# Attention and two feed-forward blocks on one core: when v and the adding transfers are issued, twelve matmuls into an idle bank, and bank locks handed back a slot later

## The chip, the cores and the metric

The kernel runs on one core of one Trainium2 chip. A core has five engines with a queue each, worked off in order: TensorE (PE, with its weight loads as PEld), VectorE (DVE), ScalarE (ACT), GpSimd (POOL) and SyncE (SP, which here only issues transfers). SP and POOL issue transfers that 16 DMA engines carry out. The metric is the device time of one execution in microseconds; lower is better.

## The reference, cut to what matters

```python
# q, k, v: (4, 8, 576, 64)
q_d, k_d, v_d = means of 4 neighbouring positions             # 144 positions
out_d     = softmax(q_d @ k_d.T / 8) @ v_d                    # coarse attention
out_local = softmax(q @ k.T / 8 where |i - j| < 4) @ v        # local attention
x  = out_d repeated 4 times + out_local                       # (4, 576, 512)
xn = (x - mean) / sqrt(var + 1e-6) * g_ln
x  = x + relu(xn @ w_ch1) @ w_ch2                             # 512 -> 2048 -> 512
xp = x shifted by one position
k  = relu((mu_k*x + (1-mu_k)*xp) @ w_k)                       # 512 -> 1024
out = sigmoid((mu_r*x + (1-mu_r)*xp) @ w_r) * ((k*k) @ w_v)   # 1024 -> 512
```

Everything is float32. The kernel keeps that precision in matmuls of a faster 32-bit type by splitting each factor into a high and a low part and adding three products (high·high, high·low, low·high): `mm3`, lines 203 to 206.

## The kernel before, in words

The 2304 positions are cut into six chunks of 384 columns, c = 0 to 5. The first half of the program goes through the chunks with the first feed-forward block (layer 1 into the banks `h_ps`, layer 2 into the four banks `acc0` to `acc3`, 16 slices f of the hidden size, 384 matmuls in a chunk). The attention of chunk c+1 is woven into the matmuls of chunk c: `slot` is called four times per slice and lets the generators in `Attn` advance by a budget. The second half (lines 773 to 837) is the second feed-forward block.

Attention of a chunk is four units (c, hp), hp being a pair of heads. A unit loads q and the windows of k (`load_qk`, tile `kz`) and the windows of v (`load_v`, tile `v`, two buffers), makes scores (coarse ones `scd`, local ones `sc`), softmaxes, transposes (`tp`, `PT`, `PdT`), multiplies with v (`av`), and adds both parts into `x`. At most two units are alive at a time. The bank `av` is shared by `scd`, `tp`, `av` and `var`; the list `av_user` in the generator is a lock on it.

The coarse k and v of a batch are sums over four neighbouring positions. For batch 0 they are made by DVE (`first_k`, tile `kf`) and POOL (`first_v`, tile `vr`). For the other batches `sums` loads one of the four parts with a transfer by SP and adds the other three with accumulating transfers issued by POOL, each of which waits until the one before it has landed (tiles `kd`, `vd`, seven buffers, lines 243 to 249). There are 12 such chains of three steps, each step a pair kd and vd: 36 pairs.

The weights come as 64-bit floats. `conv_gen` loads 32 pieces of 512 KB (`raw`, line 124, or line 129 for the last four), turns them into 32-bit floats and splits them: for each piece ACT at lines 80, 84 and 88, DVE at lines 81, 85 and 91. Piece n has to be split before the layer slice that uses it. All of it happens in front of and during chunk 0. Attention of chunk 0 has no matmuls to hide behind: it, with the first weights, is the prologue, and layer 1 of chunk 0 begins when its `x` is normalised (`xc`, `ah`, `al`).

At the end of a chunk `emit_x2` scales the four banks by the norm (`x2t`, DVE, two buffers), adds them to `x` (POOL, line 610) and stores the chunk to memory (`x2d`, one transfer of SP, line 611).

The order on each queue is set by a scheduler from its own estimate of when things are ready; an instruction given to `in_order` (line 67) keeps its place in program order among others so marked. Since queues are worked off in order, an instruction that waits holds up everything behind it on its engine. A name such as (1, 2) below is the unit hp = 2 of chunk 1.

Of the kernel before, what the change touches and what calls it, by code (L numbers as in the profile page):

```python
# [8 lines left out]
F32 = mybir.dt.float32  # L9
# [29 lines left out]
def tile_block(ctx: ExitStack, tc: tile.TileContext, qw, kw, kf, kr, vw, vr, vec, mask, w1, w2, wk, wv, wr, out):  # L39
# [27 lines left out]
    def in_order(on, ins):  # L67
        if on:
            tc.keep_in_program_order(ins)
# [37 lines left out]
    def conv_gen():  # L107
# [4 lines left out]
        def fetch():  # L112
            key = next(todo, None)
            while key in raws:
                key = next(todo, None)
            if key is None:
                return
            nm, p, k = key
            src = w1s[:, :, 1024 * p:1024 * p + 1024] if nm == "w1" else w2s[:, 4 * p:4 * p + 4, :]
            t = wpool.tile([128, 2, 1024], I32, tag="w", name="raw")  # L120
            for i in range(2):
                raws[nm, p, k + i] = t[:, i]
            for i in range(2):
                in_order(len(raws) < 18, nc.sync.dma_start(t[:, i], src[:, k + i]))

# [12 lines left out]
        for n, key in enumerate(keys + [None]):  # L138
            pin = n < PINNED
            if last:  # L140
                in_order(pin, split_hi(h, w))
            if key:
                nm, p, k = key
                W = W1 if nm == "w1" else W2
                if p not in W:
                    W[p] = wtiles(f"{nm}_{p}")
                g = decode(raws[key], pin)
                w1st = next(g)
            yield
            if key:  # L150
                next(g, None)
            if last:
                in_order(pin, split_lo(h, l, w))
                done.add(last)
            if key:
                h, l, w = W[p][0][:, k, :], W[p][1][:, k, :], w1st
            last = key
            if n % 2 == 1 or n > 24:
                fetch()
            if n + 1 < len(keys):  # L160
                fetch_late(keys[n + 1])
            yield
# [47 lines left out]
    loaded, kds, vdt, vts = {}, {}, {}, {}  # L210
    qds, adding, firsts, raw_k, means = {}, {}, [], {}, {}
    xt, xsum, stage = {}, {}, {}
# [28 lines left out]
    def sums(c, hp):  # L241

        new = [(b, *sum_tiles(b, hp)) for b in dict.fromkeys(runs(c)) if (b, hp) not in kds]
        for r in range(4):
            for b, kd, vd in new:
                eng, op = (nc.gpsimd, {"accum_op": ALU.add}) if r else (nc.sync, {})
                in_order(c <= 1 and r > 0, eng.dma_start(kd, kr[b, hp, r], **op))  # L247
                in_order(c <= 1 and r > 0, eng.dma_start(vd, vr[b, hp, r], **op))  # L248
            yield

# [15 lines left out]
    def prep(c, hp):  # L266
# [9 lines left out]
        qds[c, hp] = qd  # L276

    def mean_of(c, hp):
        if hp == 0:
# [3 lines left out]
    def unit(c, hp, nxt):  # L283
        if (c, hp) not in qds:
            prep(c, hp)
        if nxt is not None:
            if nxt not in loaded:
                load_qk(*nxt)
                if nxt[0] == 0:
                    first_k(nxt[1])  # L290
            if nxt not in vts:
                load_v(*nxt)
                if nxt[0] == 0:
                    first_v(nxt[1])
        i = units.index((c, hp)) + 2
        far = units[i] if i < len(units) else None
        if far is not None and far not in adding:
            adding[far] = sums(*far)
        step = lambda: next(adding[far], None) if far is not None else None
        step()  # L300
        new = c == 0 or runs(c)[1] != runs(c - 1)[1]
        q, k = loaded.pop((c, hp))
        v = vts.pop((c, hp))
        if hp == 0:
# [41 lines left out]
        for j in range(2):  # L346
            nc.scalar.activation(Pd[:, j, :], scd[:, j, :], AF.Exp, bias=m[:, j:j + 1], scale=0.125 / 16.0, accum_out=sm[0:2 * QB, 2 * NG + j:2 * NG + j + 1])  # L347
        if c > 0:
            av_user.clear()
        elif nxt in loaded:  # L350
            prep(*nxt)
        yield 900
        stage[c, hp] = 1
        step()
        nc.vector.tensor_reduce(mx[:, 0:2 * NG], Pl, axis=AX.X, op=ALU.max)
# [10 lines left out]
        yield 400  # L366
        step()
        nc.vector.tensor_reduce(sm[:, 0:2 * NG], P[:, :, 0:WIN + 1], axis=AX.X, op=ALU.add)
# [4 lines left out]
        while c + hp > 0 and units[units.index((c, hp)) - 1] not in multiplied:  # L373
            yield GAP
        step()
        T = pat.tile([128, 2 * NG, 32], F32, tag="T", name="T", bufs=1)
# [21 lines left out]
        if c == 0 and hp > 0:  # L398
            mean_of(c, hp - 1)
        av = ps_at.tile([128, 512], F32, tag="av", name="av")  # L400
        for n in range(NG):
# [26 lines left out]
        if c == 0:  # L428
            if hp == NHP - 1:
                mean_of(c, hp)  # L430
        elif hp == 1:
            xsum[c] = pln.tile([128, N], F32, tag="xsum", name="xsum")
# [51 lines left out]
    def scale(c):  # L484
# [26 lines left out]
        nc.vector.tensor_scalar(ve, var[:, 0:N], 1e-6, None, op0=ALU.add)  # L511
        nc.scalar.activation(t, ve, AF.Ln)
        av_user.clear()
        yield 400
        nc.scalar.activation(y, t, AF.Exp, scale=-0.5)
# [88 lines left out]
    def emit_x2(c):  # L604
        x = xt.pop(c)
        y = rstd.pop(c)
        for o in range(KT):
            t = xp.tile([128, N], F32, tag="x2", name="x2t")
            nc.vector.tensor_tensor(t, acc[o][:, 0:N], y, op=ALU.mult)  # L609
            nc.gpsimd.tensor_tensor(x[:, o, :], t, x[:, o, :], op=ALU.add)  # L610
        nc.sync.dma_start(x2d[:, :, N * c:N * c + N], x)

# [39 lines left out]
    for o in ORDER:  # L652
# [9 lines left out]
        else:  # L662
            next(conv)
    adding.update((u, iter(())) for u in units[0:NHP])
    first = Attn(None, 0)
# [244 lines left out]
```

## Time and profile before

| what | value |
|---|---|
| median of 3 runs | 795.38 us (795.38 to 796.32) |
| profiled execution | 795.89 us |
| its span, first to last instruction | 794.1 us |
| PE busy | 752.4 us, 95% of the span |
| DVE busy | 513.0 us, 65% |
| ACT busy | 370.7 us, 47% |
| POOL busy | 99.3 us, 13% |
| mean granted clock of TensorE | 0.987 of full |

Busy shares are means over stages that differ. The prologue takes the first 54 us, chunk 0 ends at about 152 us, chunk 5 at about 540 us, and the second block fills the rest. In the rows, a time at the start of a row is its start from the beginning of the span, the next number its duration; in square brackets stands how long the engine had been idle before it and what it had waited for. "SPq" is the issue of a transfer by SP. PEclk is the granted clock as a share of full speed: 1.00 is 2.4 GHz, 0.50 is 1.2 GHz.

### The profile page before, as it was taken

The page shows a single profiled execution, that of the slowest core. Times are in us where ns is not written, and L with a number is a line of the kernel's source. Part 1 is how long each engine was busy: PE and PEld are TensorE (multiplying, and loading weights), DVE is VectorE, ACT ScalarE, POOL GpSimd, SP SyncE. Part 2 cuts the span into 40 slices and gives each one's busy share as a digit, 9 for nine tenths or more (in the row PEclk, how much of TensorE's full clock was granted, in tenths as well). Part 3 has the DMA queues.
Part 4 walks back from the last instruction along what each step waited for, and adds up shares of the span by engine and source line. Part 5 has one row for each costly group of instructions (what it writes and reads, how often), then busy time and mean ns, then how long its engine had stood idle before and what let it go on. Part 6 is the DMA issues. An engine that isn't in the chain of part 4 may idle for free.

```text
span 794.1 us, 13626 instructions
## 1 busy us (share of the span) xinstructions
PE 752.4 (95%) x5380; PEld 722.6 (91%) x5380; DVE 513.0 (65%) x1015; ACT 370.7 (47%) x839; POOL 99.3 (13%) x124
## 2 busy tenths in 40 slices
PE   3669979899999999999999999999999999999998
PEld 2449869799999999999999999999999999999998
DVE  6777688766546655655555446625969596868664
ACT  4577587645434453445345324524444353525140
POOL 2334123413340001110100010001000000000000
PEclk9969999999999999999999999999999999999999
DMA  8894786446633421553134003403020202010101
GB/s 242 248 249 85 217 232 167 118 139 169 161 71 129 128 96 67 145 138 100 67 101 142 1 1 133 133 1 120 6 75 11 70 1 80 1 40 1 41 1 40
DMA packets 49023, 78.79 MB, mean 99 GB/s; under 512 B 5568, under 2 KB 34880, under 8 KB 48960
## 3 DMA queue, kind: packets, MB, share of 16 engines
q1 hardware_dynamic: 40320, 72.61, 29.0%
q0 software_dynamic: 8640, 5.32, 5.1%
q8 instruction: 42, 0.69, 0.3%
q14 instruction: 21, 0.17, 0.1%
HBM read 63.22 MB, written 14.68 MB: 98 GB/s over the span
## 4 chain that ended last, share of the span: by engine, by line
PE 83%; DMA 5%; ACT 5%; DVE 4%; issue 1%; SPq 1%; POOL 0%; ACTq 0%; POOLq 0%
PE b_ps L206 11%; PE b_ps L204 10%; PE b_ps L205 10%; PE h_ps L204 8%; PE h_ps L205 7%; PE h_ps L206 7%; PE acc L204 7%; PE acc L205 7%; PE acc L206 7%; PE av L403 2%; DMA raw<-in_w 2%; PE scd L333 1%; DMA vd<-in_vr 1%; DMA q<-in_qw 1%; PE sc L337 1%; ACT PT L381 1%
## 5 line engine op out<-in xcount | busy, mean ns | idle before, releaser
L590 DVE SCALAR_TENSOR_TENSOR hl<-h_ps,hh 128x384 fp32r<-128x384 f32 x96 | 53.0, 553 | 94.3 <-ACT hh L589 94.0
L589 ACT ACTIVATE hh<-h_ps 128x384 fp32r<-128x384 f32 x96 | 46.9, 489 | 104.3 <-PE h_ps L206 103.9
L206 PE MATMUL b_ps<-k,wbl 128*128 128x384 f32 x192 | 64.1, 334 | 0.0
L204 PE MATMUL b_ps<-xk,wbh 128*128 128x384 f32 x192 | 64.1, 334 | 0.0
L205 PE MATMUL b_ps<-xk,wbh 128*128 128x384 f32 x192 | 64.1, 334 | 0.0
L206 PE MATMUL b_ps<-xk,wbl 128*128 128x384 f32 x192 | 64.1, 334 | 0.0
L204 PE MATMUL b_ps<-k,wbh 128*128 128x384 f32 x192 | 64.1, 334 | 0.0
L205 PE MATMUL b_ps<-k,wbh 128*128 128x384 f32 x192 | 64.1, 334 | 0.0
L820 DVE RECIPROCAL e<-e 128x384 f32<-128x384 f32 x24 | 61.1, 2544 | 0.1
L610 POOL TENSOR_TENSOR x<-x2t,x 128x384 f32<-128x384 f32 x24 | 23.9, 1058 | 254.4 <-DVE x2t L609 132.2
L737 ACT ACTIVATE mixa<-x2in,vec_t 128x384 f32<-128x384 f32 x48 | 28.1, 612 | 39.7 <-DVE xr L740 33.9
L248 POOL DMA_DIRECT2D vd<-in_vr x36 | 35.1, 991 | 90.9 <-DMA vd<-in_vr 74.1
L381 ACT COPY PT<-T 32x192 f32<-32x192 f32 x96 | 33.4, 348 | 25.5 <-DVE T L377 22.9
L247 POOL DMA_DIRECT2D kd<-in_kr x36 | 35.6, 1013 | 65.8 <-DMA kd<-in_kr 60.0
L800 ACT ACTIVATE kr<-b_ps 128x384 f32<-128x384 f32 x48 | 23.5, 490 | 43.5 <-PE b_ps L206 43.5
L85 DVE SCALAR_TENSOR_TENSOR rm<-rm 128x512 uint32<-128x512 uint32 x52 | 35.7, 688 | 11.2 <-ACT rm L84 10.4
L801 DVE TENSOR_TENSOR kr<-kr,b_ps 128x384 f32<-128x384 f32 x48 | 26.5, 553 | 23.4 <-ACT kr L800 23.4
L84 ACT ACTIVATE rm<-raw 128x512 uint8<-128x512 uint8 x52 | 40.5, 784 | 2.1 <-DVE rm L81 1.9
L790 DVE TENSOR_TENSOR k<-kr,k 128x384 fp32r<-128x384 f32 x48 | 26.7, 557 | 20.3 <-ACT k L789 20.3
L347 ACT ACTIVATE Pd<-scd,mx 96x144 f32<-96x144 f32 x48 | 17.7, 372 | 44.2 <-DVE mx L344 43.7
L80 ACT ACTIVATE rm<-raw 128x512 f32<-128x512 f32 x52 | 34.3, 662 | 6.0 <-DMA raw<-in_w 5.7
L204 PE MATMUL h_ps<-ah,w_2h 128*128 128x384 f32 x96 | 34.6, 360 | 1.9 <-ACT w_2h L88 1.9
(162 smaller groups left out, 2266.6 us busy)
## 6 DMA issues: line engine op xcount, KB each, us to landing
raw<-in_w SPq DMA_DIRECT2D x32, 512.0 KB, 9.5
v<-in_vw SPq DMA_DIRECT2D x24, 256.0 KB, 2.7
bd<-rm SPq DMA_DIRECT2D x20, 256.0 KB, 2.3
wf<-bd SPq DMA_DIRECT2D x10, 512.0 KB, 3.6
q<-in_qw SPq DMA_DIRECT2D x24, 208.0 KB, 2.7
kz<-in_kw SPq DMA_DIRECT2D x48, 102.0 KB, 3.4
x2d<-x SPq DMA_DIRECT2D x6, 768.0 KB
out<-ot SPq DMA_DIRECT2D x24, 192.0 KB, 2.4
```

Of the source, the lines that this page charges most:

```text
L80: in_order(pinned, nc.scalar.activation(ru.bitcast(F32), raw.rearrange("p (n t) -> p n t", t=2)[:, :, 1].bitcast(F32), AF.Copy, scale=2.0 ...
L84: in_order(pinned, nc.scalar.activation(low, top, AF.Copy, scale=1.0 / 32.0, bias=-31.0 / 64.0))
L85: in_order(pinned, nc.vector.scalar_tensor_tensor(ru, ru, 3, m, op0=ALU.logical_shift_left, op1=ALU.bitwise_or))
L204: nc.tensor.matmul(ps, wh, ah, start=first, stop=False)
L205: nc.tensor.matmul(ps, wh, al, start=False, stop=False)
L206: nc.tensor.matmul(ps, wl, ah, start=False, stop=last)
L247: in_order(c <= 1 and r > 0, eng.dma_start(kd, kr[b, hp, r], **op))
L248: in_order(c <= 1 and r > 0, eng.dma_start(vd, vr[b, hp, r], **op))
L381: nc.scalar.copy(PT[p, :, j, :], T[p, :, 0:24])
L589: nc.scalar.activation(hh, ps[:, 0:N], AF.Relu)
L590: last_hl[0] = nc.vector.scalar_tensor_tensor(hl, ps[:, 0:N], 0.0, hh.bitcast(F32), op0=ALU.max, op1=ALU.subtract)
L820: nc.vector.reciprocal(e, e)
```

## The change: what it does

- `load_v` of the next unit moves from the start of a unit to the place where the unit before it has been multiplied with v; the same place now starts a chain of `sums` for the unit after next. Chains stand in one list and `tick`, called four times in a unit, issues one step of the first chain. All accumulating transfers keep program order, not only those of chunks 0 and 1.
- The first 8 loaded weight pieces keep program order instead of the first 16, and one more tile of two pieces is fetched at piece 4.
- `warm` puts 4 matmuls of 128 x 512 in front of the last `mean` matmul of chunk 0 and 8 behind it. They read split weights and write the bank `acc3`, which is not read before layer 2 overwrites it.
- The lock on the bank `av` is given back one slot later at two places (lines 349 and 513).
- The chunk is stored by four transfers that POOL issues, each after its add, instead of one by SP.

```diff
@@ conv_gen
-                in_order(len(raws) < 18, nc.sync.dma_start(t[:, i], src[:, k + i]))
+                in_order(len(raws) < 9, nc.sync.dma_start(t[:, i], src[:, k + i]))
...
-            if n % 2 == 1 or n > 24:
+            if n % 2 == 1 or n > 24 or n == 4:
                 fetch()
@@ sums
-                in_order(c <= 1 and r > 0, eng.dma_start(kd, kr[b, hp, r], **op))
-                in_order(c <= 1 and r > 0, eng.dma_start(vd, vr[b, hp, r], **op))
-            yield
+                in_order(r > 0, eng.dma_start(kd, kr[b, hp, r], **op))
+                in_order(r > 0, eng.dma_start(vd, vr[b, hp, r], **op))
+            if new:
+                yield True
+
+    def tick():
+        while chains and next(chains[0], None) is None:
+            chains.pop(0)
@@
+    def warm(n):
+
+        ps = ps_acc.tile([128, 512], F32, tag="acc3", name="warm")
+        w = W1[0][0]
+        for _ in range(n):
+            in_order(True, nc.tensor.matmul(ps, w[:, 0, 0:128], w[:, 0, :], start=True, stop=True))
@@ unit, at its start
-            if nxt not in vts:
-                load_v(*nxt)
-                if nxt[0] == 0:
-                    first_v(nxt[1])
-        i = units.index((c, hp)) + 2
-        far = units[i] if i < len(units) else None
-        if far is not None and far not in adding:
-            adding[far] = sums(*far)
-        step = lambda: next(adding[far], None) if far is not None else None
-        step()
+        tick()
@@ unit, after the scores
-        if c > 0:
-            av_user.clear()
-        elif nxt in loaded:
+        if c == 0 and nxt in loaded:
             prep(*nxt)
         yield 900
+        if c > 0:
+            yield GAP
+            av_user.clear()
@@ unit, after the unit before it is multiplied
-        step()
+        if nxt is not None and nxt not in vts:
+            load_v(*nxt)
+            if nxt[0] == 0:
+                first_v(nxt[1])
+        i = units.index((c, hp)) + 2
+        if NHP <= i < len(units):
+            chains.append(sums(*units[i]))
+        tick()
@@ unit, at its end
             if hp == NHP - 1:
+                warm(4)
                 mean_of(c, hp)
+                warm(8)
@@ emit_x2
-        nc.sync.dma_start(x2d[:, :, N * c:N * c + N], x)
+        for o in range(KT):
+            nc.gpsimd.dma_start(x2d[:, o, N * c:N * c + N], x[:, o, :])
```

What this does to the queues, at three places. First SP, from the load of v for unit (1, 1) to that for (1, 2). Before:

```order
L233 DMA v<-in_vw 128x512
L247 DMA kd<-in_kr 128x144
L248 DMA vd<-in_vr 72x256
L124 DMA raw<-in_w 128x1024 x4
L247 DMA kd<-in_kr 128x144
L224 DMA q<-in_qw 128x416
L228 DMA kz_104<-in_kw 64x408 x2
L233 DMA v<-in_vw 128x512
L248 DMA vd<-in_vr 72x256
L124 DMA raw<-in_w 128x1024 x6
```

Now the queue between the same two loads of v, with the four pieces of weights that stand ahead of the first:

```order
L124 DMA raw<-in_w 128x1024 x4
L233 DMA v<-in_vw 128x512
L247 DMA kd<-in_kr 128x144
L248 DMA vd<-in_vr 72x256
L124 DMA raw<-in_w 128x1024 x2
L224 DMA q<-in_qw 128x416
L228 DMA kz_104<-in_kw 64x408 x2
L124 DMA raw<-in_w 128x1024 x4
L247 DMA kd<-in_kr 128x144
L124 DMA raw<-in_w 128x1024 x2
L233 DMA v<-in_vw 128x512
```

Ahead of the load of v for (1, 2), counted from the start of the queue, stood 14 pieces of weights; now 24 do.

Second PE, the end of the prologue; the last row is the start of layer 1. Before:

```order
L412 MATMUL av<-PdT,vd 64x96 x4
L281 MATMUL mean<-x,ones_r 128x384
L392 MATMUL tp<-ident,Pd 72x96 x4
L403 MATMUL av<-PT,v 64x96 x8
L412 MATMUL av<-PdT,vd 64x96 x4
L281 MATMUL mean<-x,ones_r 128x384
L204 MATMUL h_ps<-ah,w_0h 128x384 x2
```

Now:

```order
L424 MATMUL av<-PdT,vd 64x96 x4
L403 MATMUL tp<-ident,Pd 72x96 x4
L293 MATMUL mean<-x,ones_r 128x384
L415 MATMUL av<-PT,v 64x96 x8
L424 MATMUL av<-PdT,vd 64x96 x4
L288 MATMUL warm<-w_0h 128x512 x4
L293 MATMUL mean<-x,ones_r 128x384
L288 MATMUL warm<-w_0h 128x512 x8
L204 MATMUL h_ps<-ah,w_0h 128x384 x2
```

The transposes `tp` of the last unit come one place earlier, and the twelve matmuls stand on both sides of the last mean.

Third POOL, around the adds at the end of chunk 0. Before:

```order
L247 DMA kd<-in_kr 128x144
L248 DMA vd<-in_vr 72x256
L247 DMA kd<-in_kr 128x144 x2
L248 DMA vd<-in_vr 72x256 x3
L610 TENSOR_TENSOR x<-x2t,x 128x384 x4
```

Now:

```order
L247 DMA kd<-in_kr 128x144
L248 DMA vd<-in_vr 72x256
L625 TENSOR_TENSOR x<-x2t,x 128x384
L627 DMA x2d<-x 128x384
L625 TENSOR_TENSOR x<-x2t,x 128x384 x2
L627 DMA x2d<-x 128x384
L625 TENSOR_TENSOR x<-x2t,x 128x384
L627 DMA x2d<-x 128x384 x2
```

Ahead of these adds stood 21 accumulating pairs; now 12 do, and the issue of a store stands between the first add and the second.

## Rows read from the trace of the kernel before

**Rows 1.** Busy time by stretch: length, PE, PEld, DVE, ACT, POOL, then PEclk, DMA share, GB/s.
```profile
54.00:152.00 98.00, 90.26 (x680) 81.58 (x681) 78.17 (x171) 73.34 (x156) 29.24 (x33) 0.95 0.68 181
152.00:233.00 81.00, 79.22 (x641) 75.42 (x640) 47.05 (x109) 35.93 (x91) 26.28 (x30) 1.00 0.53 134
...
500.00:600.00 100.00, 100.00 (x579) 100.00 (x578) 60.43 (x104) 41.97 (x88) 4.05 (x5) 1.00 0.19 61
```

**Rows 2.** Timeline of SP, from the prologue to chunk 0.
```profile
51.12 1.77 SPq L124 DMA_DIRECT2D raw<-in_w  x4
...
69.14 1.72 SPq L228 DMA_DIRECT2D kz<-in_kw  x2
84.16 0.33 SPq L233 DMA_DIRECT2D v<-in_vw  x1
...
84.97 3.73 SPq L124 DMA_DIRECT2D raw<-in_w  x6
```

**Rows 3.** What SP waited for in the whole span: total us, times, longest.
```profile
SPq L233 <- PE av L412: 73.1, 14, 13.4
```

**Rows 4.** Timeline of PE: four starts after a wait, chunk 0 to chunk 4.
```profile
119.05 0.28 PE L392 MATMUL tp<-ident,Pd 96*72 96x96 f32 x1 [2.12 <-ACT Pd L365]
...
150.59 0.44 PE L205 MATMUL h_ps<-al,w_0h 128*128 128x384 f32 x1 [1.49 <-DVE al L482]
158.53 0.44 PE L205 MATMUL acc<-hl,w_0h 128*128 128x384 f32 x1 [1.57 <-DVE hl L590]
411.46 0.50 PE L392 MATMUL tp<-ident,Pd 96*72 96x96 f32 x4 [0.89 <-DVE xc L511]
```

**Rows 5.** Timeline of PE: last unit of the prologue, first layer of chunk 0.
```profile
36.81 1.27 PE L333 MATMUL scd<-kd,qdz 128*96 128x144 f32 x4 [1.43 <-DVE kd L275]
...
48.25 1.55 PE L403 MATMUL av<-PT,v 128*64 128x96 f32 x16 [3.25 <-ACT PdT L395]
...
51.42 1.65 PE L281 MATMUL mean<-x,ones_r 128*128 128x384 f32 x2 [0.99 <-DVE x L421]
54.41 1.39 PE L204 MATMUL h_ps<-ah,w_0h 128*128 128x384 f32 x2 [1.34 <-ACT ah L481]
...
60.30 0.52 PE L204 MATMUL h_ps<-ah,w_0h 128*128 128x384 f32 x1
60.62 0.52 PE L205 MATMUL h_ps<-al,w_0h 128*128 128x384 f32 x1
...
62.29 0.33 PE L204 MATMUL acc<-hh,w_0h 128*128 128x384 f32 x1
```

**Rows 6.** Timeline of DVE: what stands ahead of the last unit's coarse k.
```profile
31.21 0.41 DVE L345 TENSOR_TENSOR P<-sc,mask_t 128x240 f32<-128x240 f32 x1 [0.34 <-PE sc L337]
...
32.42 1.10 DVE L272 TENSOR_REDUCE qdz<-q 64x96 f32<-64x384 f32 x2
...
36.04 0.71 DVE L275 TENSOR_REDUCE kd<-kf 128x144 f32<-128x576 f32 x1
```

**Rows 7.** Timeline of POOL: accumulating transfers, then the adds of chunk 0.
```profile
35.32 1.03 POOL L247 DMA_DIRECT2D kd<-in_kr  x1
...
50.40 1.25 POOL L247 DMA_DIRECT2D kd<-in_kr  x1
...
58.61 0.90 POOL L247 DMA_DIRECT2D kd<-in_kr  x1 [6.07 <-DMA kd<-in_kr]
...
154.57 0.84 POOL L248 DMA_DIRECT2D vd<-in_vr  x1 [2.18 <-DMA vd<-in_vr]
155.13 4.21 POOL L610 TENSOR_TENSOR x<-x2t,x 128x384 f32<-128x384 f32 x4
```

**Rows 8.** Timeline of all engines: an ordinary boundary, chunk 1 to 2.
```profile
236.14 0.56 DVE L609 TENSOR_TENSOR x2t<-acc,y 128x384 f32<-128x384 f32 x1 [0.41 <-POOL x L610]
...
237.03 0.56 DVE L590 SCALAR_TENSOR_TENSOR hl<-h_ps,hh 128x384 fp32r<-128x384 f32 x1 [0.33 <-ACT hh L589]
...
238.57 0.33 PE L205 MATMUL acc<-hl,w_0h 128*128 128x384 f32 x1
```

More of the change, by code (lines that the diff above doesn't have):

```diff
@@ L210, in tile_block @@
     loaded, kds, vdt, vts = {}, {}, {}, {}
-    qds, adding, firsts, raw_k, means = {}, {}, [], {}, {}
+    qds, chains, firsts, raw_k, means = {}, [], [], {}, {}
     xt, xsum, stage = {}, {}, {}
@@ L290, in unit @@
                     first_k(nxt[1])
-            if nxt not in vts:
-                load_v(*nxt)
-                if nxt[0] == 0:
-                    first_v(nxt[1])
-        i = units.index((c, hp)) + 2
-        far = units[i] if i < len(units) else None
-        if far is not None and far not in adding:
-            adding[far] = sums(*far)
-        step = lambda: next(adding[far], None) if far is not None else None
-        step()
+        tick()
         new = c == 0 or runs(c)[1] != runs(c - 1)[1]
         q, k = loaded.pop((c, hp))
-        v = vts.pop((c, hp))
         if hp == 0:
@@ L366, in unit @@
         yield 400
-        step()
+        tick()
         nc.vector.tensor_reduce(sm[:, 0:2 * NG], P[:, :, 0:WIN + 1], axis=AX.X, op=ALU.add)
@@ L374, in unit @@
             yield GAP
-        step()
+        if nxt is not None and nxt not in vts:
[5 more added lines that the diff above has]
+            chains.append(sums(*units[i]))
+        tick()
         T = pat.tile([128, 2 * NG, 32], F32, tag="T", name="T", bufs=1)
@@ L399, in unit @@
             mean_of(c, hp - 1)
+        v = vts.pop((c, hp))
         av = ps_at.tile([128, 512], F32, tag="av", name="av")
@@ L512, in scale @@
         nc.scalar.activation(t, ve, AF.Ln)
+        yield 400
+        yield GAP
         av_user.clear()
-        yield 400
         nc.scalar.activation(y, t, AF.Exp, scale=-0.5)
@@ L663, in tile_block @@
             next(conv)
-    adding.update((u, iter(())) for u in units[0:NHP])
     first = Attn(None, 0)
```

## The prediction

> **What bounds the kernel now.** I began with the busy times by stretch [rows 1]. From 500 us on PE is busy all the time at full clock, 579 matmuls in 100 us, so 0.173 us each: nothing in this change touches that half. Chunk 1 (152 to 233 us) has 1.8 us of idle PE. Chunk 0 (54 to 152 us) takes 98 us for the same 384 layer matmuls, with 7.7 us idle and a mean clock of 0.95. A clock that is either 1.00 or 0.50 averages 0.95 over 98 us if it is low for 9.8 us, which costs up to half of that, 4.9 us. So chunk 0 has about 12.6 us to give, the prologue in front of it 54 us in which PE mostly waits, and the rest next to nothing.
>
> The second view is SP's timeline [rows 2]. Four weight pieces go out at 51.1; the last issue before the gap ends at 70.9 (69.14 + 1.72); then SP stands until 84.16, where a load of v starts, and the next six pieces leave only at 84.97. What it stood for is v's buffer, freed by the `av` matmuls: 14 such waits, 73.1 us, the longest 13.4 [rows 3]. No weight piece left between 53 and 85 us. The third is PE's waits [rows 4]: 2.1 us at 119, for a softmax step of ACT; 1.5 at 150.6, for `al`; 1.6 at 158.5, for `hl`; 0.9 at 411. The first two lie in chunk 0 and make 3.6 of its 7.7 us; the others there are shorter. The fourth is the prologue's end [rows 5, 6], the fifth POOL [rows 7].
>
> **The change, part by part.** The sum is made against the profiled execution, 795.89 us; the median of the runs lies 0.5 below it.
>
> *Weights past the loads of v.* By the order, 24 pieces instead of 14 now stand ahead of the load of v for (1, 2), which was the one that held SP until 84. Ten pieces thus leave some 20 to 30 us earlier, while layer 1 of chunk 0 is young. Later loads of v still wait for `av`, but for that of the unit before the previous one, which is about to run when they reach the head. In chunk 0 the idle 7.7 us came when ACT and DVE caught up with pieces that had landed late; I expect 5.7 of it to go and 2 to stay. Bounds: 3 and 7.7. Of the 9.8 us at half clock, some 7.3 are the first layer's (54 to between 60.9 and 62.3, below); the other 2.5, worth 1.3 us, I put down to a clock that fell at one of this stretch's waits, the longest being that at 119 [rows 4], and take them to go with it: −1.3 (0 if the wait stays). Against this, DVE has 78.2 and ACT 73.3 us of work in this chunk [rows 1], and none of it goes. In 88 us instead of 98 DVE would be 89% busy instead of 80%, and an in-order queue that full makes new short waits: I set 2.0 us for these (0 to 4).
>
> *Prologue.* In DVE's queue the last unit's reductions of q and k now follow directly on the line 345 instruction of the unit before; that ends at 31.62, the two reductions of q take 1.10 and that of k 0.71, so k would be there at 33.4 and not at 36.75 [rows 6]: 3.3 us earlier. From this unit's scores to its product with v took 11.4 us (36.81 to 48.25) [rows 5]. If all of that moved, 3.3 us; but the previous unit's steps are pushed back behind these, and ACT gets one more piece of weights to decode ahead of `ah`. I take 2.0; bounds 3.3 and 0.
>
> *Twelve matmuls.* In the first layer a matmul starts every 0.32 us (60.30 to 60.62), half speed against 0.173, and its 24 run from 54.41 to 62.29 [rows 5]. No 128x512 matmul is in the trace; from 384 columns I estimate 0.43 us at half and 0.23 at full speed. The product with v ends at 50.43 (0.99 before the last mean, which starts at 51.42): four at half speed take 1.7 and push the mean back by 0.7. The mean ends at 53.07 (51.42 + 1.65), plus 0.7 is 53.8; eight take 3.4 at half speed, so layer 1 would start at 57.2, 2.8 us late, and if the clock rises only then as far into the work as before, nothing is won back: +2.8. In this trace a matmul of the first layer lasts 0.52 us at 60.62 and 0.33 at 62.29, so the clock rose after 6 to 8 us of nearly unbroken work from 54.41 [rows 5]. With the extra matmuls it works without a break from 50.4, so the rise falls near 56 to 58, or earlier as the last unit's products add to it; I put it at 55; layer 1 then starts at about 56 and its 24 matmuls take 4.2 us at full speed, a little more as `al` arrives one slice at a time: done at 60.7 instead of 62.3. That is −1.6. Bounds +2.8 and −3.5 (24 times 0.147, nothing lost in front). I take −1.6, the middle course that the order of events in this trace gives.
>
> *POOL.* The adds of chunk 0 started at 155.13, right behind an accumulating transfer issued at 154.57 that had waited for the one ahead of it [rows 7]; `hl` stood behind `x2t` on DVE and PE lost 1.57 us [rows 4]. With 12 pairs ahead instead of 21 the queue is through long before: −1.6 (0 if something else holds them). The price is at every boundary: the issue of a store, 0.84 us or a little more [rows 7], now stands between the first add and the second, and the last `x2t` starts as much later. At an ordinary boundary that one ran from 236.14 to 236.70, `hl` ended at 237.59 and was wanted at 238.57 [rows 8]. Shifted by 0.9 the `x2t` ends at 237.60, `hl` at 238.16: 0.4 us are left, cost 0. SP no longer waits for the adds; that only helps the loads of q behind it.
>
> *Later chunks.* The scores of chunk 4's units now stand at other places; the wait of 0.89 at 411 [rows 4] may go or stay: −0.45. The locks given back a slot later put no unit's end later than about 42 layer matmuls (7.3 us) ahead of the next chunk, which the mean, four `xc` and the first `al` fit into: 0.
>
> Sum: −5.7 −1.3 +2.0 −2.0 −1.6 −1.6 −0.45 = −10.65. Profiled 785.2, median 784.7.
>
> **A page against it.** The stores of x2d are plain transfers moved to POOL. POOL's 0.84 us an issue [rows 7] is the price taken above. The Trainium skill, in "DMA: Bandwidth & Descriptors", section "SWDGE vs HWDGE vs iDMA", advises SP or ACT for plain transfers, since POOL writes descriptors in software through memory ports that VectorE can lock it out of. By that rule the issues stretch while DVE is busy, and the store rival below applies; the rows decide for the short price, having 0.84 to 1.25 us beside a busy DVE [rows 7].
>
> **Rivals.**
> 1. *Conversion bounds chunk 0.* For it: DVE 78.2 and ACT 73.3 us busy in 98, dependent on each other three times per piece. Against: no piece left before 85 us, so both had to catch up in the second half of the chunk. If DVE can be only 82% full, chunk 0 shrinks to 95 us, 3 less with the first layer in it; with −1.6 at the boundary: 795.4 − 4.6 = 790.8.
> 2. *Accumulating transfers become the wait (slower).* The units' scores come up to 30 layer matmuls (5 us) earlier, and now the weights fill the DMA engines while the chains run. First chain: 35.32 to 50.40, 5.0 us a step; the longest step, 50.40 to 58.61, took 8.2 [rows 7]. Scores of (1, 2) are due, by their place 195 layer matmuls into chunk 0, at 195 × 0.173 = 34 us plus some 9 us of attention and low clock after about 52: near 95. Nine steps start about 2.5 us later than before, at 38. At 5.0 they end at 83, 12 us in time; above 6.3 a step they are late; at 8.2 they end at 112, 17 us late, which takes the place of the gain: 784.7 + 17 = 802. It decides for slower from about 7.5 a step. Against it: 5.0 was the mean under a full load already.
> 3. *Stores on POOL.* If an issue took 2 us, each of five boundaries lost 0.7 to 1.1 us: about +5, 789.7.
> 4. *It doesn't do what it says.* The scheduler's place for the pieces helps nothing, since their buffers free up late, or what is gained in front is lost at the drain before chunk 1: 795.
>
> **How the numbers follow.** Forecast 0.64, with an own range of 777.5 to 790; rival 1 0.18, rival 2 0.08, rival 3 0.04, rival 4 0.06. The low end: everything at its good bound is −3.3 −3.5 −7.7 −1.3 −1.6 −0.9 = −18.3, 777.1, which wants all at once; I stop at 777.5. The high end: prologue 0, first layer +2.8, chunk 0 −3 −1.3, crowding +2, boundary −1.6 and nothing at 411 is −1.1; I stop at 793.5, holding rival 1 and leaving rivals 2 and 4 out. A difference of 0.2% (1.6 us) is about what a measurement of this kernel can tell from none. Faster: 0.64 + 0.18 + 0.04 and 0.01 of rival 4, 0.87; same 0.05; slower 0.08.
>
> **What would show it.** In SP's timeline, no gap without weight pieces between 55 and 85 us. In chunk 0's stretch, idle PE near 2 to 4 us with one low-clock stretch fewer, and a length near 88 us. In the first layer, steps of 0.17 from the first slice on. The product with v of the prologue's last unit near 46. At 150 us, POOL's adds right behind `x2t`. The prediction is wrong if PE waits at `scd` for an accumulating transfer, if the steps of 0.32 last as long behind the added matmuls, or if DVE in chunk 0 is above 90% with the chunk still over 94 us.

## The result: 1.7% faster, most of it in chunk 0

The changed kernel takes 781.73 us (median of 4 runs, 780.69 to 783.32) against 795.38; the ratio is 0.9828, 95% interval 0.9807 to 0.985. The forecast was 784.7, with a range of 777.5 to 793.5. The profiled execution spans 779.1 us instead of 794.1. From its page, busy time by engine and then the granted clock in 40 slices (what its first slices are worth is said in the last section):

```profile
PE 746.8 (96%) x5392; PEld 721.2 (93%) x5392; DVE 512.3 (66%) x1015; ACT 370.6 (48%) x839; POOL 113.0 (15%) x148
...
PEclk9869999999999999999999999999999999999999
```

Chunk 0 runs from the first matmul of layer 1 to the first `x2t`, the others from `x2t` to `x2t`. In the trace of before chunk 0 lasted 98.2 us (54.41 to 152.64), now 85.6 (55.53 to 141.09); its end lies 11.5 us earlier. Chunk 1 is 1.8 us shorter (80.84 to 79.06), chunk 4 1.5 (80.66 to 79.15); what is left, 0.2, is spread over the rest. The stretches that answer to [rows 1], columns as there:

```profile
55.50:141.00 85.50, 83.45 (x680) 77.50 (x679) 75.95 (x168) 70.72 (x152) 14.39 (x16) 1.00 0.61 172
141.00:220.00 79.00, 79.00 (x644) 76.06 (x643) 45.94 (x108) 35.65 (x91) 11.48 (x14) 1.00 0.39 119
500.00:600.00 100.00, 100.00 (x579) 100.00 (x578) 67.01 (x106) 40.99 (x84) 6.21 (x9) 1.00 0.12 40
```

Read them in order. In chunk 0 PE is idle for 2.05 us (85.50 − 83.45) instead of 7.7, and the clock is 1.00 throughout instead of 0.95, worth some 4.9 us. DVE's work hardly changed (75.95 after 78.17), so it is 89% busy, as forecast. The two together explain about 10.5 of the 12.6 us; the other 2 are in PE's busy time, and no row says where. In chunk 1 no idle is left.

SP's timeline for the same stretch, to set beside [rows 2]:

```profile
46.25 2.26 SPq L124 DMA_DIRECT2D raw<-in_w  x4
...
52.87 1.44 SPq L124 DMA_DIRECT2D raw<-in_w  x2
67.21 1.12 SPq L228 DMA_DIRECT2D kz<-in_kw  x2
68.44 2.54 SPq L124 DMA_DIRECT2D raw<-in_w  x4
...
71.78 1.04 SPq L124 DMA_DIRECT2D raw<-in_w  x2
82.59 0.33 SPq L233 DMA_DIRECT2D v<-in_vw  x1
```

Six pieces leave between 68 and 73 us (they are the 19th to the 24th, which had left between 87 and 97), ahead of the load of v that stood at 84.16 before and stands at 82.59 now: that load waits as it did, but the pieces are no longer behind it. The four pieces before them, which had left at 85 to 87 us, now leave at 47 to 54. From there to 68 us no piece leaves, so the gap is shorter and not gone. SP's waits over the whole span show the same: that for `av` (line 412 before [rows 3], 424 now) fell from 73.1 to 43.8, and another, for `sc`, became the largest in total of SP's attention waits:

```profile
SPq L224 <- PE sc L339: 65.4, 18, 16.4
...
SPq L233 <- PE av L424: 43.8, 15, 9.9
```

PE's waits in chunk 0 are now these three, 1.83 us together; the four of [rows 4] are gone and nothing above 0.15 us stands at their places:

```profile
85.51 0.73 PE L335 MATMUL scd<-kd,qdz 128*96 128x144 f32 x4 [0.73 <-DVE x L433]
...
100.98 0.73 PE L335 MATMUL scd<-kd,qdz 128*96 128x144 f32 x4 [0.66 <-DVE x L433]
...
116.74 0.73 PE L335 MATMUL scd<-kd,qdz 128*96 128x144 f32 x4 [0.44 <-DVE x L433]
```

The prologue's end on PE, beside [rows 5]:

```profile
33.18 0.73 PE L335 MATMUL scd<-kd,qdz 128*96 128x144 f32 x4 [0.86 <-DVE kd L280]
...
48.57 1.55 PE L415 MATMUL av<-PT,v 128*64 128x96 f32 x16 [3.23 <-ACT PT L392]
...
50.69 2.04 PE L288 MATMUL warm<-w_0h 128*128 128x512 f32 x4
52.94 0.91 PE L293 MATMUL mean<-x,ones_r 128*128 128x384 f32 x2 [0.22 <-DVE x L433]
53.40 2.30 PE L288 MATMUL warm<-w_0h 128*128 128x512 f32 x8
55.53 0.81 PE L204 MATMUL h_ps<-ah,w_0h 128*128 128x384 f32 x2
...
60.35 0.33 PE L204 MATMUL acc<-hh,w_0h 128*128 128x384 f32 x1
```

The last unit's scores come 3.6 us earlier (33.18 after 36.81), its product with v 0.3 later (48.57 after 48.25), and its mean 1.5 later (52.94 after 51.42). What holds the mean is DVE's queue; its rows just ahead of the `x` that the mean waited for:

```profile
51.13 0.69 DVE L85 SCALAR_TENSOR_TENSOR rm<-rm 128x512 uint32<-128x512 uint32 x1
51.73 0.68 DVE L91 TENSOR_TENSOR w_0l<-rm,w_0h 128x512 fp32r<-128x512 f32 x1
52.34 0.55 DVE L433 TENSOR_TENSOR x<-av,ud 128x384 f32<-128x384 f32 x1
```

Pieces of weights are split where `x` should be made; on ACT too, which copies the product for it (`ud`) at 51.89, a microsecond after PE was done. At the end of chunk 0, POOL, beside [rows 7]:

```profile
141.73 1.01 POOL L625 TENSOR_TENSOR x<-x2t,x 128x384 f32<-128x384 f32 x1 [43.27 <-DVE x2t L624]
143.15 0.61 POOL L627 DMA_DIRECT2D x2d<-x  x1 [0.41 <-POOL x L625]
143.78 2.00 POOL L625 TENSOR_TENSOR x<-x2t,x 128x384 f32<-128x384 f32 x2
145.69 0.59 POOL L627 DMA_DIRECT2D x2d<-x  x1
...
147.25 1.09 POOL L627 DMA_DIRECT2D x2d<-x  x2
```

It had been idle for 43 us, so no transfer held the adds. At the next boundary, chunk 1 to 2 as in [rows 8]:

```profile
223.90 0.56 DVE L624 TENSOR_TENSOR x2t<-acc,y 128x384 f32<-128x384 f32 x1 [1.51 <-POOL x L625]
224.38 0.55 DVE L605 SCALAR_TENSOR_TENSOR hl<-h_ps,hh 128x384 fp32r<-128x384 f32 x1
```

The last `x2t` waits 1.51 instead of 0.41 us for its buffer, yet `hl` ends at 224.93 and the matmul that takes it starts at 225.23 without a wait.

### The profile page after: what moved, and what is told of

The parts are those of the page before. It is cut to its first block, busy times and chain, and to the rows that moved or that the text cites. A ratio compares the mean times of both kernels' runs of the same rounds, so it can differ in the third digit from the quotient of the medians.

```text
span 779.1 us, 13662 instructions
## 1 busy us (share of the span) xinstructions
PE 746.8 (96%) x5392; PEld 721.2 (93%) x5392; DVE 512.3 (66%) x1015; ACT 370.6 (48%) x839; POOL 113.0 (15%) x148
## 4 chain that ended last, share of the span: by engine, by line
PE 86%; ACT 6%; DVE 5%; DMA 1%; issue 1%; SPq 0%; ACTq 0%; DVEq 0%
PE b_ps L206 11%; PE b_ps L204 11%; PE b_ps L205 11%; PE acc L204 8%; PE h_ps L204 8%; PE acc L205 8%; PE acc L206 8%; PE h_ps L206 7%; PE h_ps L205 7%; PE av L415 2%; PE sc L339 2%; PE scd L335 2%; ACT rm L84 1%; DVE rm L85 1%; ACT rm L80 1%; PE av L424 1%
## 5 line engine op out<-in xcount | busy, mean ns | idle before, releaser
L248 POOL DMA_DIRECT2D vd<-in_vr x36 | 38.9, 1086 | 21.9 <-DMA vd<-in_vr 15.4
L204 PEld LDWEIGHTS b_ps<-xk,wbh 128*128 128x128 f32 x192 | 36.0, 188 | 0.0
L205 PEld LDWEIGHTS b_ps<-xk,wbh 128*128 128x128 f32 x192 | 36.0, 188 | 0.0
```

What stands on the lines that cost most here:

```text
L204: nc.tensor.matmul(ps, wh, ah, start=first, stop=False)
L205: nc.tensor.matmul(ps, wh, al, start=False, stop=False)
L248: in_order(r > 0, eng.dma_start(vd, vr[b, hp, r], **op))
```

## The experiments

All ratios are to the kernel before on the same chip. The changed kernel itself, measured again beside three of these, gave 782.81 us, ratio 0.9829 (0.9799 to 0.9858), and a span of 780.8; its first layer began at 57.46 where the first profile had 55.53. So a single span carries some 2 us of noise from the prologue, about half of it from slower matmuls just ahead of layer 1 (see the run without the twelve), and chunk lengths say more than spans. In the table, + is a part of the change put into the kernel before, − a part taken out of the changed kernel; each row's lengths are from one profile:

| kernel | layer 1 starts | chunk 0 ends | chunk 1 | chunk 4 | span | ratio |
|---|---|---|---|---|---|---|
| before | 54.41 | 152.64 | 80.84 | 80.66 | 794.1 | 1 |
| + fetch lines | 55.11 | 146.12 | 79.85 | 80.92 | 786.8 | 0.9883 |
| + loads of v | 54.98 | 155.34 | 80.92 | 81.11 | 797.3 | 1.0051 |
| + twelve matmuls | 55.24 | 152.22 | 81.70 | 80.48 | 794.4 | 0.9983 |
| + locks | 55.45 | 146.45 | 78.64 | 79.14 | 784.2 | 0.9858 |
| changed | 55.53 | 141.09 | 79.06 | 79.15 | 779.1 | 0.9828 |
| changed, again | 57.46 | 142.75 | 79.06 | 79.14 | 780.8 | 0.9829 |
| − twelve matmuls | 55.61 | 142.47 | 79.08 | 79.13 | 780.5 | 0.9828 |
| − adding transfers | 52.37 | 143.93 | 79.84 | 79.13 | 782.7 | 0.9849 |
| − locks | 59.54 | 144.42 | 80.47 | 80.51 | 785.2 | 0.9859 |
| − fetch lines | 54.71 | 139.21 | 79.08 | 79.14 | 777.2 | 0.9788 |
| − fetch lines, − loads of v | 53.06 | 142.07 | 79.15 | 79.13 | 780.2 | 0.9842 |
| − stores on POOL | 58.36 | 143.44 | 78.96 | 79.15 | 781.5 | 0.9827 |
| − fetch lines, fewer ahead | 52.12 | 143.63 | 77.25 | 79.14 | 779.8 | 0.9826 |

### Parts of the change put into the kernel before

**The fetch lines alone.**

```diff
-                in_order(len(raws) < 18, ...)
+                in_order(len(raws) < 9, ...)
-            if n % 2 == 1 or n > 24:
+            if n % 2 == 1 or n > 24 or n == 4:
```

> The kernel before with the edits to the fetching of weights alone (8 pinned pieces instead of 16, one tile more at piece 4); loads of v, chains, locks, stores as before, no extra matmuls. By its order 24 pieces stand ahead of the load of v for (1, 2), where the kernel before has 14. Theory 'pieces': what shortened chunk 0 is that the pieces leave earlier, whichever edit does it. Then the gap without pieces between 53 and 85 us goes, the waits of PE between 94 and 119 us go with the low clock behind them, and the time falls by 7 to 9 us, to about 787; the waits at the start of chunk 1 (1.5 and 1.6 us) and the half clock of the first layer stay. Rival 'loads of v': SP's head of the line is what counts, and that is not touched: 795, no change. Rival 'attention': chunk 0 got shorter because attention's steps stand earlier in PE's queue; these stand only half as far forward here (mean at 354 layer matmuls against 356 before and 342 now): at most 2 us, 793.

Measured: 788.08 us, ratio 0.9883 (0.9861 to 0.9904). SP's timeline in this kernel:

```profile
75.30 3.86 SPq L124 DMA_DIRECT2D raw<-in_w  x6
87.89 0.33 SPq L233 DMA_DIRECT2D v<-in_vw  x1
```

Six pieces leave just ahead of the load of v, 24 in all from the start of the queue. Chunk 0 becomes 7 us shorter although the code of the loads of v is as before, and although its first layer has a new wait of 3.08 us, for an `xc` (at 58.88).

**The loads of v alone.**

```diff
@@ unit, at its start
-            if nxt not in vts:
-                load_v(*nxt)
@@ unit, after the unit before it is multiplied
+        if nxt is not None and nxt not in vts:
+            load_v(*nxt)
...
```

Not shown are the lines that take `v` out of `vts` later, at its use, and the `first_v` lines that go with `load_v`.

> The kernel before with the loads of v alone moved behind the previous unit's product. By its order 14 pieces of weights still stand ahead of the load of v for (1, 2). Theory 'pieces': no change, 794 to 796, with the gap without pieces still there. Rival 'loads of v' (my prediction's wording): the gap goes, 787 or less.

Measured: 799.2 us, ratio 1.0051 (1.0028 to 1.0074): 0.5% slower. The gap in SP's timeline stays, and six pieces follow the load of v as in [rows 2]:

```profile
87.06 0.33 SPq L233 DMA_DIRECT2D v<-in_vw  x1
...
87.88 3.77 SPq L124 DMA_DIRECT2D raw<-in_w  x6
```

Its waits in chunk 0 are those of before (2.45 us at 121.96 instead of 2.12 at 119.05), and one of 2.98 in the first layer is new, for an `xc` that stands on DVE behind the splitting of weights. So moving the loads of v alone does not free SP.

**The twelve matmuls alone.**

```diff
             if hp == NHP - 1:
+                warm(4)
                 mean_of(c, hp)
+                warm(8)
```

> The kernel before with the twelve matmuls alone. Theory 'clock': clock at 1.00 from about 53 us, first layer done 1.6 to 2 us earlier. Theory 'pieces' adds that this is then lost again while chunk 0 waits for weights: the wait at 119 and those before grow by as much, and the total is 794.5 to 795.4. Rival 'kept': all of it reaches the end, 793.5.

Measured: 795.59 us, ratio 0.9983 (0.9966 to 0.9999). The granted clock is 1.00 from 54 to 117 us and the first layer ends at 60.37 instead of 62.29, but chunk 0 ends only 0.4 earlier: the waits for late pieces take the rest back. Behind the wait that ends at 118.05 (2.04 us) the clock is low once more, with a mean of 0.66 from 117 to 122.

**The locks alone.**

```diff
-        if c > 0:
-            av_user.clear()
-        elif nxt in loaded:
+        if c == 0 and nxt in loaded:
             prep(*nxt)
         yield 900
+        if c > 0:
+            yield GAP
+            av_user.clear()
@@ norm
-        av_user.clear()
         yield 400
+        yield GAP
+        av_user.clear()
```

> The kernel before with nothing changed but the places where the bank locks are given back. By the order this alone puts 21 pieces of weights, not 14, ahead of the load of v for (1, 2), and the mean of chunk 0's last unit at layer matmul 342, not 356. Theory (locks are the main lever; the prediction put them at 0): chunk 0 shrinks by 6 to 9 us, chunks 1 and 4 by 1.0 to 1.5 each (79.1 to 79.8 instead of 80.8 and 80.7), span 783 to 786, ratio 0.984 to 0.989. Rival (the fetch lines are the lever, the locks matter only beside them): gain of at most 3, from chunks 1 and 4, span 791 or more, ratio 0.996 or above.

Measured: 785.25 us, ratio 0.9858 (0.9835 to 0.9882), the largest gain of any part, though its interval overlaps that of the fetch lines (0.9861 to 0.9904). SP's timeline:

```profile
72.63 3.22 SPq L124 DMA_DIRECT2D raw<-in_w  x5
85.05 0.33 SPq L233 DMA_DIRECT2D v<-in_vw  x1
```

Five pieces leave just ahead of the load of v with neither the fetch lines nor the loads of v touched: the scheduler puts 21 ahead of it once the attention steps lie otherwise. Why it does is not seen in a trace and stays open. Chunk 0 is 91.0 us long then, as with the fetch lines alone (both from the table). Chunks 1 and 4 shrink by 2.2 and 1.5 us besides. What this kernel has in chunk 0 and the changed one has not is the low clock of the first layer (0.50 up to 62 us, a mean of 0.96 in the chunk) and these waits:

```profile
119.58 0.73 PE L333 MATMUL scd<-kd,qdz 128*96 128x144 f32 x4 [1.29 <-DVE x L422]
...
132.83 0.88 PE L404 MATMUL av<-PT,v 128*64 128x96 f32 x16 [1.84 <-ACT PdT L396]
```

### Parts taken out of the changed kernel

**Without the twelve matmuls** (the two calls of `warm` removed).

> The changed kernel without the twelve extra matmuls. Theory 'clock': first layer at half clock again for 5 to 7 us, but begun 1 us earlier (about 54.4 instead of 55.5): 1.6 to 2 us slower than the changed kernel, 783.5. Rival 'clock rises anyway': layer 1 starts 1 us earlier and at full clock: 780.7. Rival 'no matter': chunk 0 has slack and takes the difference up: 781.7.

Measured: 783.73 us, ratio 0.9828 (0.9808 to 0.9849), as with them. The first layer's matmuls last 0.52 us until 59, and the layer takes 6.29 us (55.61 to 61.90) where the changed kernel took 4.82 (55.53 to 60.35); the chunk ends 1.4 later. But the second profile of the changed kernel, twelve matmuls included, ended its first layer at 61.93, no earlier than this one. There the layer took 4.47 us, but began late, at 57.46, and eight of the twelve are part of the reason:

```profile
54.67 2.96 PE L288 MATMUL warm<-w_0h 128*128 128x512 f32 x8
```

In the first profile they took 2.30 (53.40, above), at a granted clock of 1.00 throughout; here the clock rose only at 56.04, while they ran. What the twelve give to the layer they can take in front of it, so no gain of theirs is shown in the end.

**With the old adding transfers.**

```diff
-        tick()
+        i = units.index((c, hp)) + 2
+        far = units[i] if i < len(units) else None
+        if far is not None and far not in adding:
+            adding[far] = sums(*far)
+        step = lambda: next(adding[far], None) if far is not None else None
+        step()
...
```

Not shown are the other calls of `tick`, which become `step()`, and the old lines of `sums`.

> The changed kernel with the old adding transfers: each unit's chain is a generator of its own, advanced at fixed places two units ahead, and 21 pairs stand on POOL ahead of chunk 0's adds of x2. Theory (the prediction's POOL term): the adds wait for the accumulating transfer ahead of them again, hl stands behind x2t, and a PE wait of about 1.6 us returns shortly after the first x2t; profiled span 779.1 + 1.6 = 780.7, ratio to the kernel before about 0.985. Rival: with chunk 0 tuned by the other edits the 21 pairs have landed before the adds at 141 (at 5 us a step from 36, two chains deep, they end near 130), the adds start right behind x2t, no wait comes back, span 779 +- 0.5.

Measured: 784.34 us, ratio 0.9849 (0.9817 to 0.9882); its runs overlap those of the changed kernel on this chip (782.65 to 788.0 beside 781.86 to 784.47). The adds stand behind the last accumulating transfer again:

```profile
144.44 0.83 POOL L248 DMA_DIRECT2D vd<-in_vr  x1 [2.04 <-DMA vd<-in_vr]
145.00 1.33 POOL L622 TENSOR_TENSOR x<-x2t,x 128x384 f32<-128x384 f32 x1
```

The first add starts 1.07 us after `x2t` (143.93) instead of 0.64, PE waits 0.37 for `hl` at 149.55, and chunk 1 is 0.8 longer. The mechanism is there; its size is about half of what was expected. In chunk 0 most is lost elsewhere: a wait of 3.56 us for `xc` in the first layer, at 56.37.

**With the locks given back as before** (the diff above, reversed).

> The changed kernel with the bank locks given back at the old places. Theory: the attention steps of chunk 0 take their banks 12 to 14 layer matmuls otherwise, the mean of the last unit of chunk 0 comes at 354 instead of 342 of 384, so al of the next chunk comes late and the wait of before at the chunk's end (1.49 us) and that of chunk 4 (0.89 us) come back in part: span 780 to 781.5, ratio 0.984 to 0.986. Rival (the prediction's value for this edit, 0): the places move but nothing waits there, span 779 +- 0.5.

Measured: 785.68 us, ratio 0.9859 (0.9826 to 0.9892); the runs lie at 783.97 to 786.98, the changed kernel's beside them at 781.86 to 784.47. Chunks 1 and 4 go back to 80.47 and 80.51, almost the 80.84 and 80.66 of before, with waits at the transposes:

```profile
162.86 0.50 PE L402 MATMUL tp<-ident,Pd 96*72 96x96 f32 x4 [0.45 <-DVE xc L524]
...
402.44 0.50 PE L402 MATMUL tp<-ident,Pd 96*72 96x96 f32 x4 [0.48 <-DVE xc L524]
```

A second wait, for `Pd`, follows in each (0.59 at 179.30, 0.50 at 418.76). In chunk 4 the first is the wait of before in part, as expected ([rows 4], 0.89 at 411.46); in chunk 1 they stand at the transposes, and not at `al`. Some 2.8 us (1.41 and 1.36), then, are the locks' own, beside the pieces; the rival that valued them at nothing is out.

**With the old fetch lines** (the first diff, reversed).

> The changed kernel with the scheduler's old rule for weight pieces (18 pinned in order, no extra fetch at n = 4). By the order 21 pieces still stand ahead of the load of v for (1, 2), against 14 in the kernel before and more in the changed one. Theory (what counts is how many pieces stand ahead of that load): most of the gain stays, span 780 to 783, ratio 0.983 to 0.987. Rival (the two fetch lines alone carry the gain, as fetch alone gave 0.988 and loads of v alone 1.005): chunk 0 goes back to about 96 us, span 788 or more, ratio 0.993 or above.

Measured: 779.4 us, ratio 0.9788 (0.9759 to 0.9818). Each of its runs (779.01 to 781.21) is below each of the changed kernel's on this chip. So the fetch lines, which gain 1.2% alone, cost 0.4% beside the locks, which already put 21 pieces ahead. In the changed kernel two further pieces are issued at 33 us; that they are what is in the prologue's way was not tested by itself, but the end of the prologue fits it. ACT copies the last unit's `ud` at 50.28 instead of 51.89, and DVE makes its `x` at 50.55 instead of 52.34:

```profile
49.98 0.42 DVE L81 TENSOR_SCALAR rm<-rm 128x512 uint32<-128x512 uint32 x1
50.55 0.56 DVE L433 TENSOR_TENSOR x<-av,ud 128x384 f32<-128x384 f32 x1
```

In chunk 0 one wait above 0.3 us is left (0.48 at 99.36) where the changed kernel has three, and the chunk itself is 84.5 us long instead of 85.6 and 85.3 in its two profiles.

**The changed kernel again, unchanged,** on one chip with the three kernels above it.

> The changed kernel itself, beside the three others on one chip, as their measure: ratio 0.983 to the kernel before, span 779 +- 1.

Measured: 782.81 us, as said at the head of this section.

**With the old fetch lines and the old place for the loads of v.**

> The changed kernel with the old fetch rules and the loads of v back at the start of a unit, so that only locks, adding transfers, stores and warm matmuls are changed. By the order 20 pieces stand ahead of the load of v for (1, 2), against 21 with the loads moved. Theory (where the loads of v stand is worth nothing once the locks have put the pieces ahead of them): the same as with the fetch rules alone undone, span 777 to 779, ratio 0.978 to 0.981. Rival (the prediction's wording: the loads of v have to be late to free SP): SP stands at v(1, 1) and v(1, 2) from about 55 to 80, chunk 0 is 4 to 8 us longer, span 781 to 785, ratio 0.984 or above.

Measured: 784.88 us, ratio 0.9842 (0.9815 to 0.9869), 0.5% above the kernel with the old fetch lines alone (another chip). The theory fell in its number, the rival in its mechanism: SP does not hold the pieces back (eight leave at 48.57, four at 71.31, ahead of the load at 84.48). Lost is a wait in the first layer, on PE:

```profile
53.06 0.34 PE L204 MATMUL h_ps<-ah,w_0h 128*128 128x384 f32 x1
56.56 0.45 PE L204 MATMUL h_ps<-ah,w_0h 128*128 128x384 f32 x1 [3.16 <-DVE xc L486]
```

The reason is DVE's order; its timeline in the same kernel just before:

```profile
54.75 0.69 DVE L85 SCALAR_TENSOR_TENSOR rm<-rm 128x512 uint32<-128x512 uint32 x1
55.35 0.68 DVE L91 TENSOR_TENSOR w_0l<-rm,w_0h 128x512 fp32r<-128x512 f32 x1
55.95 0.55 DVE L486 TENSOR_TENSOR xc<-x,mean 128x384 f32<-128x384 f32 x1
```

The last `xc` stands behind operations of the weights. The same wait, of 3.0 to 3.6 us, is in four kernels here (fetch lines alone, loads of v alone, old adding transfers, this one) and not in the changed kernel, where the four `xc` run together. In all four, operations of the weights stand on DVE between the first `xc` and the last, so it depends on where the scheduler puts them.

**With the store on SP.**

```diff
-        for o in range(KT):
-            nc.gpsimd.dma_start(x2d[:, o, N * c:N * c + N], x[:, o, :])
+        nc.sync.dma_start(x2d[:, :, N * c:N * c + N], x)
```

> The changed kernel with the store of x2 as one transfer on SP again. Theory (the prediction's value 0 for the stores on POOL): the adds of a boundary follow one another without 0.6 us of issue between, the four x2t start over 2.8 us instead of 3.7, PE waited for neither, span 779 to 781, ratio 0.983. Rival (stores on POOL cost at every boundary, rival 3 of the prediction): each of five boundaries gains 0.3 to 0.9 us, span 775 to 777.5, ratio 0.979.

Measured: 782.78 us, ratio 0.9827 (0.9802 to 0.9853), no difference. The four `x2t` of chunk 0 start within 2.66 us (143.44 to 146.10) instead of 3.75, and no matmul profits. Theory right, rival out.

**A candidate: old fetch lines, fewer weights split ahead.**

```diff
-        if i >= PRO0 and i % 10 in (0, 3, 6):
+        if i >= PRO0 and i % 10 in (0, 5):
```

The first diff, reversed, goes with it.

> The changed kernel with the old fetch rules, and in the prologue a piece of weights converted at two of ten steps instead of three, so that fewer conversions stand on DVE ahead of the x of the prologue's last unit. Theory (in the prologue the last product with v and the mean wait for DVE, which is busy with pieces of weights): the first layer starts at 53 to 54 instead of 55.5, and as DVE is about 90% full in chunk 0 it takes the pieces over without a wait: span 774 to 777. Rival (DVE sets the length of chunk 0: what is not converted in front is paid there): chunk 0 ends where it did or later, 139 to 142, span 777 to 780.

Measured: 783.07 us, ratio 0.9826 (0.9803 to 0.985), 0.4% above the old fetch lines alone, with intervals that overlap and on another chip. The first layer does start earlier, at 52.12, but chunk 0 ends at 143.63, with PE waiting for weights:

```profile
74.40 0.45 PE L204 MATMUL h_ps<-ah,w_1h 128*128 128x384 f32 x1 [0.86 <-ACT w_1h L88]
...
96.56 0.44 PE L204 MATMUL h_ps<-ah,w_2h 128*128 128x384 f32 x1 [0.44 <-ACT w_2h L88]
```

What is not split in the prologue is paid in chunk 0: the rival, and more than it said. The edit also delays the loads: only 16 pieces leave ahead of the load of v for (1, 2), instead of 21, and this run does not part the two. The best version measured is the changed kernel with the old fetch lines.

## Why the prediction was right, and which steps of it were not

**What bounds the kernel.** Right. Chunk 0 was taken to have 12.6 us to give and became 12.6 shorter; from chunk 5 on nothing moved. That the two numbers are equal is chance: 2 us of idle stayed, and 2 came out of PE's busy time, which the sum did not have.

**Weights past the loads of v (−5.7, clock −1.3, crowding +2.0).** The mechanism was right, the edit behind it not. Ten more pieces stand ahead of that load of v and leave some 19 to 37 us earlier than before, idle PE falls to the 2 us that were forecast, and the clock stays up: the trace of before has it at 0.50 from 119.3 to 122.6, right behind the wait that the prediction named, and now it is 1.00 there. But the count of 24 pieces came from the order of the whole changed kernel, and the prediction did not ask which edit had made it. It is not the loads of v, which alone change nothing in that place and cost 0.5%; the locks alone do it (−1.4%, later chunks included), the fetch lines alone do it (−1.2%), and one makes the other needless. The step that failed is its price of 0 for the locks: it looked at how late a unit would end, and not at what moves in the queues when attention shifts. The term of +2.0 for crowding was too large: DVE did reach the 89%, its three new waits make 1.83 us, and they stand inside the 2 us of idle already counted.

**Prologue (−2.0).** Wrong: nothing came of it. The last unit's scores moved by the full 3.3 us and a little more, and its product with v did not move at all. The risk had been named, that steps and pieces of weights are pushed behind; it took everything. Layer 1 starts at 55.53, 1.1 later than before. Without the twelve matmuls it starts at 55.61 too, and its last mean at 52.61 after 51.42, having waited for DVE's `x`; so DVE's order is reason enough. In other profiles the twelve add to it, as said next.

**Twelve matmuls (−1.6).** The mechanism was right, the gain is not steady. Behind them the first layer takes 4.82, 4.47 and 4.16 us (changed, again, with the store on SP) instead of 6.29 without them and 7.88 before. But they stand in front of it, and when they run at half speed the eight take up to 3.90 us (store on SP) instead of 2.30. The layer then ended at 61.93 and 62.52, against 60.35 in the first profile and 61.90 without them. That is the bad course, which the prediction priced with layer 1 at 57.2 and kept as a bound (it began at 57.46 and 58.36, 0.8 of which was there at the product with v); the −1.6 of the first profile is luck in part. The timed runs show no gain (0.9828 with and without).

**POOL (−1.6, stores 0).** The 1.57 us of [rows 4] are gone, and the adds wait for no transfer. But with the locks alone they are gone too, 21 pairs and all: there the last issue came 0.45 us after `x2t` (146.90 after 146.45), not 1.93 as before (154.57 after 152.64). With the old transfers in the changed kernel 0.37 comes back. So the pairs can hold the adds, and how long depends on when the last one lands; this edit's own share is between 0 and 0.8 us. The stores cost nothing, as said. The 0.84 us taken for an issue was that of an accumulating transfer at 154.57, and not beside a busy DVE, as the prediction has it: DVE was idle for 2.85 us until 156.50. The first two stores of chunk 0 took 0.61 and 0.59, with DVE idle most of that time; the last two, 1.09 together at 147.25, while DVE was in one `xc` from 146.92 to 148.15. The lock-out that the Trainium skill warns of ("DMA: Bandwidth & Descriptors", section "SWDGE vs HWDGE vs iDMA"), and ties to one mode of VectorE, is not seen in these rows; none of them tells VectorE's mode, so they do not test it.

**Later chunks (−0.45).** Too small: −1.5 in chunk 4, and −1.8 in chunk 1, of which 1.6 had been booked under POOL. Taking the locks back returns 1.4 in each.

**The sum.** Up to the end of the first layer 1.9 us were gained where 3.6 had been forecast (the prologue's term); in the second profile it was 0.4. From there to the end of chunk 0 it was 9.6 for 5.0: the 2.0 for crowding did not come, and some 2.5 more lay in PE's busy time, where no row shows it. Behind chunk 0 it was 3.5 for 2.05 (the locks). Together −15.0 in the profile and −13.7 in the median, after −10.65. So the total is nearer than its terms: 1.7 too much in front stood against 4.6 and 1.4 too little behind.

**The rivals.** Rival 1 put DVE's limit at 82% of chunk 0: it ran at 89% with 1.83 us of waits. Rival 2: the accumulating transfers started 4.9 us apart (36.34 to 65.55 in six steps), and no score waited for one. Rival 3: no store delayed a matmul. Rival 4: the pieces do come earlier, and it pays.

## What to carry to other kernels

When queues are filled by a scheduler, read what an edit does to every queue, not only to the one that it names: here two lock releases in the attention moved the weight loads past a blocked load and were worth as much there as the edit of the fetching itself (chunk 0 is 91.0 us long with either alone). An order of the whole change tells that something moved; only the order of each edit alone tells which one moved it, and it can be read before anything runs. Parts that gain the same thing do not add: two edits of 1.2% and 1.4% made 1.7% with all the others, and without one of them 2.1%.

## Not expected of the hardware

The mean granted clock of the whole span reads 0.987 in the changed kernel and 1.00 in the one with the store on SP. On the latter's page every slice is full (1.00 is 2.4 GHz), but its matmuls in the prologue are slow:

```profile
PEclk9999999999999999999999999999999999999999
...
33.20 1.27 PE L335 MATMUL scd<-kd,qdz 128*96 128x144 f32 x4 [0.75 <-DVE kd L280]
...
54.63 3.90 PE L288 MATMUL warm<-w_0h 128*128 128x512 f32 x8
```

The same scores took 0.73 us in the changed kernel, at 33.18 and a granted clock of 1.00, and the same eight matmuls 2.30. So this prologue ran at the lower level (1.2 GHz). Its trace has no entry of the clock before 58.03 us, and a stretch without an entry is shown as 1.00. The changed kernel's trace has none before 25.24 us: the product with v at 17.20 lasts 1.54 us under a reading of 1.00, and 1.55 at 48.57 under one of 0.50. A reading of 1.00 in a prologue, and a run's mean clock of 1.00, is therefore to be set beside how long the matmuls last.

The kernel with the store on SP started its first layer at 58.36, not at 55.53: its product with v came 0.8 us later (49.38 after 48.57), and the clock rose at 58 us instead of 52.55, so that the last mean and the eight matmuls in front of the layer were slow. That is no effect of the store: the changed kernel's own second profile has the rise at 56.04. Why it comes at another time from one execution to the next was not found.

A plain store issued by POOL takes 0.54 to 0.61 us in the changed kernel, an accumulating transfer 0.83 to 0.92 where the timelines here show one alone.
